# Causal attention with a 64-row tail before two feed-forward layers: the tail rows padded to 128 in the transposes and the product with the values

## The chip, the cores and the metric

The kernel runs on one core of one Trainium2 chip. The metric is the device time of one execution in microseconds (us), the median of three runs. The engines are TensorE (PE, whose weight loads the trace keeps apart as PEld), VectorE (DVE), ScalarE (ACT) and GpSimd (POOL); SyncE (SP) issues the DMAs.

## The reference

Attention over 4 batches, 8 heads, 576 positions and 64 features per head, with a causal mask and a bias from a running sum of `max(s, 0)`; then two feed-forward layers over the 2304 tokens, 512 to 2048 to 512. All of it is in float32.

```python
def _attn_ref(q, k, v, s):
    scale = 1.0 / np.sqrt(D)
    scores = scale * np.matmul(q, k.transpose(0, 1, 3, 2))
    cum = np.cumsum(np.maximum(s, 0.0), axis=-1)
    bias = -(cum[:, :, :, None] - cum[:, :, None, :])
    scores = np.where(causal, -1000000000.0, scores + np.minimum(bias, 0.0))
    scores = scores - np.max(scores, axis=-1, keepdims=True)
    attn = np.exp(scores)
    attn = attn / (np.sum(attn, axis=-1, keepdims=True) + 1e-09)
    return np.matmul(attn, v)
...
    x = attn_out.transpose(0, 2, 1, 3).reshape(B * S, H * D)
    h = x @ w_in                                  # first layer
    x = (h * np.clip(h + 3.0, 0.0, 6.0) / 6.0) @ w_out
    h = x @ w2_in                                 # second layer
    return (h * (1.0 / (1.0 + np.exp(-h)))) @ w2_out
```

## The kernel before

576 positions are four chunks of 128 and a fifth of 64 (`CH`, line 52). Each head is worked in two parts: part A holds the queries 0 to 255 (chunks 0 and 1), part B the queries 256 to 575 (chunks 2, 3 and 4; chunk 4 has 64 rows). So there are 32 heads of part A (`A0_0` to `A3_7`) and 32 of part B (`B0_0` to `B3_7`), taken in the order A0 A1 A2 B0 A3 B1 B2 B3 (line 198), eight heads each. Most arithmetic on float32 is done with a high and a low half (`th`, `tl`; `xh`, `xl`; `gh`, `gl`), each of a format that TensorE multiplies in one pass.

A head of part B goes through these stages. `score` (line 468) multiplies queries with keys into the PSUM tiles `ps0` to `ps3`. `soft` (487) adds the mask `cmask` and finds the row minimum, on DVE, and writes the rows of chunk c to the tile `pb2`, `pb3` or `pb4`. `expo` (500) takes the exponentials on ACT. `norm` (511) divides by the sums: a small sum and a reciprocal on DVE, then one multiplication per chunk on POOL. `trans` (525) transposes the probabilities on TensorE, so that keys come to lie on partitions. It works by groups of key chunks, `[0, 3]`, `[1, 4]` and `[2]` (line 355); one group fills one of two PSUM banks (`pt0`, `pt1`, `pt2`, from the pool `ps_t`). ACT copies the bank to `th`, and `trans_low` (559) subtracts on DVE and leaves `tl`. `v_high` and `v_low` (435, 442) split the values into `vs`, the first on DVE and the second on POOL. `av` (563) multiplies `vs` with `th` and `tl` into the PSUM tile `po`, chunk of keys by chunk of keys; ACT and DVE move the result on.

What has 64 rows on the contracted side of TensorE: the transposes of `pb4`, whose stationary operand is `pb4` itself (five of the twelve transposes of a head; for key chunk 4 it is 64 by 64), and the two products of `av` for key chunk 4. A row of the trace shows this as `64*128` or `64*64` (rows * columns of the stationary operand).

`slot` (688) writes one head's score stage, the transposes and `av` of the head before, and one step of the first feed-forward layer (`first`, `gate_high`, `gate_low`, `second`: the tiles `ph`, `g`, `gh`, `gl`, `acc`) in one piece of code. The order on each engine is not the order of the code: a scheduler in the compiler sets it, and so it can change wherever an instruction changes. After the last head come the rest of the first layer and the whole second layer, in which no head is worked.

Of the kernel before, what the change touches and what calls it, by code (L numbers as in the profile page):

```python
# [22 lines left out]
def f32(ap):  # L23
    return ap.bitcast(F32)
# [3 lines left out]
def kernel(  # L28
# [42 lines left out]
    make_identity(nc, ident)  # L71


    cmask = cpool.tile([P, NFULL * P + P], F32, tag="cmask", name="cmask")
    nc.gpsimd.memset(cmask, 0.0)
    nc.gpsimd.affine_select(
        out=cmask[:, NFULL * P :], in_=cmask[:, NFULL * P :], pattern=[[-1, P]],
        compare_op=ALU.is_ge, fill=-1e9 / SCALE, base=0, channel_multiplier=1,
    )
    half = cpool.tile([P, 1], F32, tag="half", name="half")  # L80
# [207 lines left out]

    c1 = ctx.enter_context(ExitStack())
    apool = c1.enter_context(tc.tile_pool(name="apool", bufs=1))  # L290
    c2 = c1.enter_context(ExitStack())

    def psum(name, bufs):
# [47 lines left out]
    class Head:  # L341
# [3 lines left out]
        def __init__(self, b, part, h, whole, at):  # L345
            self.b, self.part, self.h, self.whole, self.at = b, part, h, whole, at
            self.slot = at % 2
            self.bh = b * H + h
            self.nm = f"{part}{b}_{h}"
            self.chunks = [c for c in range(NCH) if (CH[c][0] < T1) == (part == "A")]  # L350
            self.q0 = CH[self.chunks[0]][0]
            self.nk = CH[self.chunks[-1]][0] + CH[self.chunks[-1]][1]
            self.nq = self.nk - self.q0
            self.nkc = self.chunks[-1] + 1
            self.groups = [[0, 1]] if part == "A" else [[0, 3], [1, 4], [2]]
            self.prob, self.PT, self.pt, self.pS, self.rest = {}, {}, {}, {}, []
            self.pieces = []
            for c in self.chunks:
                w = CH[c][0] + CH[c][1]
                self.pieces += [(c, 0, w, True)] if w <= 512 else [  # L360
                    (c, 0, w // 2, False), (c, w // 2, w, True)]
# [73 lines left out]
        def v_high(self):  # L435
            if self.whole:
                return
            self.vs = apool.tile([P, self.nkc, 2, D], F32R, tag="vs", name=f"vs{self.nm}")
            for cs, n in self.v_parts():
                copy("v", self.vs[:n, cs, 0, :], self.va[:n, cs, :])  # L440

# [11 lines left out]
        def places(self):  # L453
            self.sums = allsums[self.at % 4]
            self.mx = apool.tile([P, NCH + 1], F32, tag="mx", name=f"mx{self.nm}", bufs=4)
            for c in self.chunks:
                r0, n = CH[c]
                w = r0 + n
                name = f"pb{c}{self.nm}"
                if self.at < 14 and self.at % 4 > 1:  # L460
                    tag = (("qs", "kh"), ("vs", "kl"))[self.at % 4 - 2][c]
                    pb = apool.tile([P, w], F32, tag=tag, name=name)
                else:
                    tag = ("pb2", "pb3", "pb2", "pb3", "pb4")[c]
                    pb = apool.tile([P, w], F32, tag=tag, name=name, bufs=2)
                self.prob[c] = pb
# [20 lines left out]
        def soft(self, i):  # L487

            c, a, z, last = self.pieces[i]
            r0, n = CH[c]  # L490
            m0 = NFULL * P - r0
            pb = self.prob[c]
            nc.vector.tensor_tensor_reduce(
                out=pb[:n, a:z], in0=self.pS.pop(i)[:n, :], in1=cmask[:n, m0 + a : m0 + z],
                scale=-SCALE,
                scalar=BIG if a == 0 else self.mx[:n, i - 1 : i],
                op0=ALU.add, op1=ALU.min, accum_out=self.mx[:n, i : i + 1],
            )

        def expo(self, i):  # L500
            c, a, z, last = self.pieces[i]
            if not last:
                return
            n = CH[c][1]
            pb = self.prob[c]
            nc.scalar.activation(
                pb[:n, :], pb[:n, :], AF.Exp, bias=self.mx[:n, i : i + 1], scale=-1.0,
                accum_out=self.sums[:n, c : c + 1],
            )

        def norm(self):
            sm = self.sums[:, self.chunks[0] : self.nkc]
            nc.vector.tensor_scalar(out=sm, in0=sm, scalar1=1e-9, scalar2=None, op0=ALU.add)
            nc.vector.reciprocal(sm, sm)
            if self.whole:
                return
            for c in self.chunks:
                n = CH[c][1]
                pb = self.prob[c]
                nc.gpsimd.tensor_scalar(  # L520
                    out=pb[:n, :], in0=pb[:n, :], scalar1=self.sums[:n, c : c + 1], scalar2=1.0,
                    op0=ALU.mult, op1=ALU.mult,
                )

        def trans(self, gi):

            pt = bank("t", [P, 512], f"pt{gi}{self.nm}")
            off, evac = 0, []
            for kc in self.groups[gi]:
                k0, kn = CH[kc]  # L530
                start = off
                for c in self.chunks:
                    n = CH[c][1]
                    if c >= kc:
                        nc.tensor.transpose(  # L535
                            pt[:kn, off : off + n], self.prob[c][:n, k0 : k0 + kn],
                            ident[:n, :n],
                        )
                        off += n
                self.PT[kc] = (kn, start, off)  # L540
                if evac and evac[-1][0] == kn:
                    evac[-1] = (kn, evac[-1][1], off)
                else:
                    evac.append((kn, start, off))
            dt = F32 if self.whole else F32R
            tag = ("th", "tl")[self.whole and self.slot]
            hi = apool.tile([P, off], dt, tag=f"{tag}{gi}", name=f"th{gi}{self.nm}")
            self.pt[gi] = []
            if not self.whole:
                lo = apool.tile([P, off], dt, tag=f"tl{gi}", name=f"tl{gi}{self.nm}")  # L550
            for kn, a, z in evac:
                copy("a", hi[:kn, a:z], pt[:kn, a:z])
                if not self.whole:
                    self.pt[gi].append((lo[:kn, a:z], pt[:kn, a:z], hi[:kn, a:z]))
            for kc in self.groups[gi]:
                kn, a, z = self.PT[kc]
                self.PT[kc] = (hi[:kn, a:z],) if self.whole else (hi[:kn, a:z], lo[:kn, a:z])

        def trans_low(self, gi):
            for lo, pt, hi in self.pt.pop(gi):  # L560
# [2 lines left out]
        def av(self):  # L563
            b, h, nm, nq = self.b, self.h, self.nm, self.nq
            p = h // 2
            if self.whole:
                self.av_whole()
                return
            if h % 2 == 0:
                if self.part == "A":  # L570
                    xA[b, p] = apool.tile(
                        [P, T1], F32, tag=f"xA{p}", name=f"xA{b}_{p}", bufs=1
                    )
                else:
                    xB[b, p] = apool.tile(
                        [P, T1], F32, tag=f"xB{p}", name=f"xB{b}_{p}", bufs=2
                    )
                    if b == 0:
                        xZ[p] = apool.tile([P, B * TAIL], F32, tag=f"xZ{p}", name=f"xZ{p}")
            mine, other = (slice(0, D), slice(D, 2 * D))[:: 1 if h % 2 == 0 else -1]  # L580
            if self.part == "A":
                outs = [(xA[b, p], 0, T1)]
            else:
                outs = [(xB[b, p], 0, T1), (xZ[p][:, b * TAIL : (b + 1) * TAIL], T1, nq)]
            po = bank("o", [P, nq], f"po{nm}")
            for kc in range(self.nkc):
                kn = CH[kc][1]
                a = max(CH[kc][0] - self.q0, 0)
                v, o = self.vs[:kn, kc].rearrange("p a d -> p (a d)"), po[:, a:]
                last = len(self.PT[kc]) - 1  # L590
                for i, pT in enumerate(self.PT[kc]):
                    nc.tensor.matmul(  # L592
                        o, v, pT, start=kc == 0 and i == 0, stop=kc == self.nkc - 1 and i == last
                    )
            tmp = apool.tile([P, nq], F32, tag="tl2", name=f"tmp{nm}")
            nc.scalar.copy(tmp[mine, :], po[other, :])
            self.rest = [(x[mine, :], po[mine, a:z], tmp[mine, a:z]) for x, a, z in outs]
# [90 lines left out]
    def slot(cur, p1, p2, nx, loads, mm, tk=(0, 0, 0, 0)):  # L688
# [57 lines left out]
        transposed(2)  # L746
        if mm:
            gate_low(step)
        ticks(tk[3])
        if nx:  # L750
            nx.places()
# [212 lines left out]
```

## Time and profile before

| what | value |
|---|---|
| device time, median of 3 runs | 1087.41 us (1085.73 to 1089.71) |
| the profiled execution's own time | 1087.48 us |
| its span, first to last instruction | 1085.7 us |
| PE busy | 1054.0 us, 97% of the span |
| PEld busy | 943.6 us, 87% |
| DVE, ACT, POOL busy | 599.6, 431.7 and 272.5 us (55%, 40%, 25%) |
| granted TensorE clock, mean | 0.998 of full speed |

The span is what the trace covers; 1.8 us of the execution lie around it. Matmuls are pipelined: one takes some 0.28 us from start to end while the next begins 0.12 us after it, so what one costs in a stream is read from start to start, and a PE that is busy all the time can still be slowed.

### The profile page before, as it was taken

How to read it: one execution, taken by the hardware profiler on the slowest of the kernel's cores; microseconds unless marked ns; L12 is line 12 of the kernel's file. 1: busy time of each engine (PE TensorE's matmuls, PEld its weight loads, DVE VectorE, ACT ScalarE, POOL GpSimd, SP SyncE). 2: the span in 40 equal slices, each digit the busy share in tenths (PEclk: the TensorE clock that was granted, in tenths of full speed). 3: DMA queues.
4: the chain of work that ended last, by engine and by line, in shares of the span. 5: the costliest groups of instructions: out<-in, count | busy, mean ns of one | idle time of the engine just before them, and what ended most of it. 6: DMA issues, size and time to landing. Idle time of an engine off the chain costs nothing.

```text
span 1085.7 us, 18479 instructions
## 1 busy us (share of the span) xinstructions
PE 1054.0 (97%) x6658; PEld 943.6 (87%) x6658; DVE 599.6 (55%) x1549; ACT 431.7 (40%) x965; POOL 272.5 (25%) x436
## 2 busy tenths in 40 slices
PE   4988999999999999999999999999999999999998
PEld 3877899999999988988989999888888888888897
DVE  6799976776777777667754229995311311111111
ACT  5787744454445545445442117763111111111111
POOL 4000133332243344434432013232211211111110
PEclk9999999999999999999999999999999999999999
DMA  4792221222222222211201329620200100010010
GB/s 146 224 335 83 58 69 50 61 60 56 78 57 55 75 61 58 75 50 54 83 13 40 98 72 325 190 75 1 78 1 1 59 1 1 1 39 1 1 39 20
DMA packets 51426, 77.09 MB, mean 71 GB/s; under 512 B 11796, under 2 KB 34312, under 8 KB 51336
## 3 DMA queue, kind: packets, MB, share of 16 engines
q1 hardware_dynamic: 51336, 75.92, 22.6%
q8 instruction: 53, 0.87, 0.3%
q14 instruction: 37, 0.30, 0.1%
HBM read 65.93 MB, written 9.95 MB: 70 GB/s over the span
## 4 chain that ended last, share of the span: by engine, by line
PE 84%; DVE 5%; DMA 5%; POOL 2%; SPq 2%; ACT 1%; issue 1%; DVEq 0%; ACTq 0%; POOLq 0%
PE ph L231 12%; PE ph L233 11%; PE ph L232 11%; PE acc L280 6%; PE acc L281 6%; PE acc L282 6%; PE acc L277 5%; PE acc L276 5%; PE acc L278 5%; PE poB L592 5%; PE pt0B L535 3%; DMA rawo<-in_w1o_dram 2%; PE pt1B L535 1%; DMA rawi<-in_w1i_dram 1%; PE pt2B L535 1%
## 5 line engine op out<-in xcount | busy, mean ns | idle before, releaser
L254 DVE TENSOR_TENSOR gl<-g,gh 128x512 fp32r<-128x512 f32 (+1 forms) x152 | 102.7, 676 | 278.0 <-POOL gh L92 277.9
L92 POOL TENSOR_SCALAR gh<-g 128x512 fp32r<-128x512 f32 x136 | 103.1, 758 | 473.6 <-ACT g L249 303.1
L231 PE MATMUL ph<-xh,wi 128*128 128x256 f32 x576 | 169.1, 294 | 8.1 <-DVE g L245 7.8
L232 PE MATMUL ph<-xl,wi 128*128 128x256 f32 x576 | 165.9, 288 | 0.0
L233 PE MATMUL ph<-xh,wi 128*128 128x256 f32 x576 | 165.7, 288 | 0.0
L276 PE MATMUL acc<-gh,wo 128*128 128x256 f32 x576 | 162.3, 288 | 2.3 <-POOL gh L92 2.2
L277 PE MATMUL acc<-gl,wo 128*128 128x256 f32 x576 | 164.0, 287 | 0.3 <-DVE gl L254 0.2
L278 PE MATMUL acc<-gh,wo 128*128 128x256 f32 x576 | 162.9, 285 | 0.0
L249 ACT ACTIVATE g<-ph 128x512 f32<-128x512 f32 x72 | 42.9, 598 | 284.9 <-PE ph L233 284.8
L231 PEld LDWEIGHTS ph<-xh,wi 128*128 128x128 f32 x576 | 111.2, 193 | 11.6 <-DVE g L245 8.9
L233 PE MATMUL ph<-x2h,wi 128*128 128x512 f32 (+1 forms) x320 | 117.7, 368 | 0.0
L232 PE MATMUL ph<-x2l,wi 128*128 128x512 f32 (+1 forms) x320 | 117.7, 368 | 0.0
L231 PE MATMUL ph<-x2h,wi 128*128 128x512 f32 (+1 forms) x320 | 117.7, 368 | 0.0
L280 PE MATMUL acc<-wo,gh 128*128 128x512 f32 x288 | 112.3, 390 | 0.0
L277 PEld LDWEIGHTS acc<-gl,wo 128*128 128x128 f32 x576 | 109.9, 191 | 2.7 <-DVE gl L254 1.4
L281 PE MATMUL acc<-wo,gh 128*128 128x512 f32 x288 | 112.2, 390 | 0.0
L232 PEld LDWEIGHTS ph<-xl,wi 128*128 128x128 f32 x576 | 111.5, 194 | 0.7
L276 PEld LDWEIGHTS acc<-gh,wo 128*128 128x128 f32 x576 | 108.8, 191 | 3.8 <-POOL gh L92 2.4
L233 PEld LDWEIGHTS ph<-xh,wi 128*128 128x128 f32 x576 | 111.5, 194 | 0.7
L278 PEld LDWEIGHTS acc<-gh,wo 128*128 128x128 f32 x576 | 109.8, 191 | 1.0
L282 PE MATMUL acc<-wo,gl 128*128 128x512 f32 x288 | 101.4, 389 | 0.0
L244 ACT ACTIVATE g<-ph,half 128x512 f32<-128x512 f32 (+1 forms) x80 | 51.3, 642 | 63.2 <-PE ph L233 57.8
(185 smaller groups left out, 2102.6 us busy)
## 6 DMA issues: line engine op xcount, KB each, us to landing
k2B<-in_kT_dram SPq DMA_DIRECT2D x64, 144.0 KB
rawi<-in_w1i_dram SPq DMA_DIRECT2D x16, 512.0 KB
rawo<-in_w1o_dram SPq DMA_DIRECT2D x16, 512.0 KB
rawi<-in_w2i_dram SPq DMA_DIRECT2D x16, 512.0 KB
rawo<-in_w2o_dram SPq DMA_DIRECT2D x16, 512.0 KB
q2B<-in_qT_dram SPq DMA_DIRECT2D x64, 80.0 KB
out_dram<-o SPq DMA_DIRECT2D x18, 256.0 KB
vaB<-in_v_dram SPq DMA_DIRECT2D x32, 128.0 KB
```

Source lines behind the costliest of these rows:

```text
L92: nc.gpsimd.tensor_scalar(out=o, in0=i, scalar1=1.0, scalar2=1.0, op0=ALU.mult, op1=ALU.mult)
L231: nc.tensor.matmul(o, wih[:, cs], xh[c], start=c == 0, stop=False)
L232: nc.tensor.matmul(o, wih[:, cs], xl[c], start=False, stop=False)
L233: nc.tensor.matmul(o, wil[:, cs], xh[c], start=False, stop=c == NDC - 1)
L254: nc.vector.tensor_tensor(out=gl, in0=g, in1=f32(gh), op=ALU.subtract)
L276: nc.tensor.matmul(a, woh[:, cs], gh[:, jj, :], start=b0, stop=False)
L277: nc.tensor.matmul(a, woh[:, cs], gl[:, jj, :], start=False, stop=False)
L278: nc.tensor.matmul(a, wol[:, cs], gh[:, jj, :], start=False, stop=b1)
L280: nc.tensor.matmul(a, gh[:, jj, cs], woh, start=b0, stop=False)
L281: nc.tensor.matmul(a, gh[:, jj, cs], wol, start=False, stop=False)
L282: nc.tensor.matmul(a, gl[:, jj, cs], woh, start=False, stop=b1)
L592: nc.tensor.matmul(o, v, pT, start=kc == 0 and i == 0, stop=kc == self.nkc - 1 and i == last)
```

## The change

The rows 64 to 127 of chunk 4 are filled with zeros once, in two new tiles `last0` and `last1` of 128 by 640 that take the place of `pb4` for heads with an even and an odd number. The transposes of chunk 4 then read all 128 partitions and write 128 columns, of which only 64 are kept: the next transpose of the bank writes over the others. In `vs` the rows 64 to 127 of key chunk 4 are set to zero for each head, by a memset on POOL ahead of `v_high`, and `av` contracts over 128 rows for every key chunk. The groups become `[0, 4]`, `[1]`, `[2]`, `[3]`: four banks are filled instead of three, and one copy and one subtraction cover a whole bank. `cmask` is 512 columns wide instead of 640.

```diff
+    NKP = NCH * P
+    lasts = []
+    for i in range(2):
+        lasts.append(apool.tile([P, NKP], F32, tag=f"last{i}", name=f"last{i}"))
+        nc.gpsimd.memset(lasts[i], 0.0)
...
-            self.groups = [[0, 1]] if part == "A" else [[0, 3], [1, 4], [2]]
+            self.groups = [[0, 1]] if part == "A" else [[0, 4], [1], [2], [3]]
...
+            if self.nkc > NFULL:
+                nc.gpsimd.memset(f32(self.vs[CH[-1][1] :, NFULL]), 0.0)
             for cs, n in self.v_parts():
                 copy("v", self.vs[:n, cs, 0, :], self.va[:n, cs, :])
...
-                if self.at < 14 and self.at % 4 > 1:
+                if n < P:
+                    pb = lasts[self.slot]
+                elif self.at < 14 and self.at % 4 > 1:
...
-            m0 = NFULL * P - r0
+            m0 = -a if z <= r0 else NZ - r0
...
                     if c >= kc:
+
                         nc.tensor.transpose(
-                            pt[:kn, off : off + n], self.prob[c][:n, k0 : k0 + kn],
-                            ident[:n, :n],
+                            pt[:, off : off + P], self.prob[c][:, kc * P : (kc + 1) * P], ident
                         )
                         off += n
...
             hi = apool.tile([P, off], dt, tag=f"{tag}{gi}", name=f"th{gi}{self.nm}")
+            copy("a", hi, pt[:, :off])
...
-            for kn, a, z in evac:
-                copy("a", hi[:kn, a:z], pt[:kn, a:z])
-                if not self.whole:
-                    self.pt[gi].append((lo[:kn, a:z], pt[:kn, a:z], hi[:kn, a:z]))
+                self.pt[gi].append((lo, pt[:, :off], hi))
...
-                kn = CH[kc][1]
                 a = max(CH[kc][0] - self.q0, 0)
-                v, o = self.vs[:kn, kc].rearrange("p a d -> p (a d)"), po[:, a:]
+                v, o = self.vs[:, kc].rearrange("p a d -> p (a d)"), po[:, a:]
...
         transposed(2)
         if mm:
             gate_low(step)
+        transposed(3)
```

How the order on the engines moves is shown at three places of heads of batch 2. First, on TensorE before the change, the end of `av` of head `B2_0` (products with the values, `poB2_0`), the next head's scores `ps2B2_2` and the first transposes of `B2_1`; the last figures are the size of the output.

```order
L592 MATMUL poB2_0_5722<-th0B2_0_5624,vsB2_0_5605 128x192
L592 MATMUL poB2_0_5722<-tl0B2_0_5625,vsB2_0_5605 128x192
L592 MATMUL poB2_0_5722<-th1B2_0_5669,vsB2_0_5605 128x64
L592 MATMUL poB2_0_5722<-tl1B2_0_5670,vsB2_0_5605 128x64
L480 MATMUL ps2B2_2_5763<-kaB2_2_5553,qaB2_2_5552 64x288
...
L535 MATMUL pt0B2_1_5772<-ident_78,pb4B2_1_5551 128x64
L535 MATMUL pt0B2_1_5772<-ident_78,pb3B2_1_5550 128x128
L535 MATMUL pt0B2_1_5772<-ident_78,pb4B2_1_5551 128x64
L535 MATMUL pt1B2_1_5818<-ident_78,pb4B2_1_5551 128x64
L535 MATMUL pt1B2_1_5818<-ident_78,pb4B2_1_5551 64x64
```

On TensorE after the change, the same place: the end of `av` of `B2_0`, the transposes of `B2_1`.

```order
L598 MATMUL poB2_0_5775<-tl3B2_0_5753,vsB2_0_5655 128x192
L598 MATMUL poB2_0_5775<-th0B2_0_5674,vsB2_0_5655 128x64
L598 MATMUL poB2_0_5775<-tl0B2_0_5676,vsB2_0_5655 128x64
L549 MATMUL pt1B2_1_5871<-ident_78,pb2B2_1_5600 128x128
...
L549 MATMUL pt0B2_1_5826<-ident_78,last1_106 128x128 x2
L549 MATMUL pt1B2_1_5871<-ident_78,last1_106 128x128
...
L549 MATMUL pt2B2_1_5896<-ident_78,pb2B2_1_5600 128x128
...
L549 MATMUL pt3B2_1_5905<-ident_78,pb3B2_1_5601 128x128
L549 MATMUL pt3B2_1_5905<-ident_78,last1_106 128x128
```

The products of key chunk 4 come from `th0` and `tl0` now, the transposes of chunk 4 read `last1` with 128 rows, and a fourth bank, `pt3`, is filled after `pt2`. Ahead of the first transposes of `B0_0` and behind the end of the last head the order on TensorE does not move.

Second, on POOL after the change, around the split of the values of `B2_2`:

```order
L533 TENSOR_SCALAR last0_104<-last0_104,sums2_94 64x576
L93 TENSOR_SCALAR gh45_6009<-g45_6008 128x512
L448 MEMSET vsB2_2_5968 64x128
L458 TENSOR_TENSOR vsB2_2_5968<-vaB2_2_5837,vsB2_2_5968 128x4x64
L458 TENSOR_TENSOR vsB2_2_5968<-vaB2_2_5837,vsB2_2_5968 64x64
L93 TENSOR_SCALAR qaB2_4_5915<-q2B2_4_5865 64x320
L533 TENSOR_SCALAR pb2B2_3_5913<-pb2B2_3_5913,sums3_96 128x384
```

The memset stands right ahead of the two subtractions of `v_low`; behind it are `qa` of a later head and the multiplications of `norm`. Before the change the same piece reads:

```order
L520 TENSOR_SCALAR pb4B2_2_5704<-pb4B2_2_5704,sums2_94 64x576
L92 TENSOR_SCALAR gh45_5953<-g45_5952 128x512
L92 TENSOR_SCALAR qaB2_4_5859<-q2B2_4_5812 64x320
L448 TENSOR_TENSOR vsB2_2_5912<-vaB2_2_5784,vsB2_2_5912 128x4x64
L448 TENSOR_TENSOR vsB2_2_5912<-vaB2_2_5784,vsB2_2_5912 64x64
L92 TENSOR_SCALAR gh46_6107<-g46_6106 128x512
```

Here `qa` stood ahead of the split; now it stands behind it.

## Rows read from the trace of the kernel before

**Rows 1.** Page, part 1: busy us (share of the span) xinstructions of each engine

```profile
PE 1054.0 (97%) x6658; PEld 943.6 (87%) x6658; DVE 599.6 (55%) x1549; ACT 431.7 (40%) x965; POOL 272.5 (25%) x436
```

**Rows 2.** Windows: stretch, its us, busy us of each engine, PEclk, DMA share, GB/s

```profile
0.00:135.50 135.50, 110.12 (x657) 99.81 (x658) 116.62 (x365) 98.96 (x243) 19.81 (x63) 0.99 0.53 170
135.50:575.70 440.20, 439.97 (x3266) 404.97 (x3265) 308.83 (x908) 210.37 (x518) 162.81 (x262) 1.00 0.21 61
575.70:1085.70 510.00, 503.95 (x2738) 438.85 (x2738) 174.12 (x277) 122.36 (x206) 89.91 (x111) 1.00 0.16 54
```

**Rows 3.** Timeline of PE, 402 to 418 us: start, us, engine, line, operation, tiles, rows*columns, form

```profile
402.62 0.27 PE L535 MATMUL pt2B<-ident,pb2B 128*128 128x128 f32 x1
402.73 0.27 PE L535 MATMUL pt2B<-ident,pb3B 128*128 128x128 f32 x1
402.94 0.27 PE L535 MATMUL pt2B<-ident,pb4B 64*128 64x64 f32 x1
403.14 0.41 PE L592 MATMUL poB<-tl0B,vsB 128*128 128x320 f32 x1
403.39 0.31 PE L592 MATMUL poB<-th1B,vsB 128*128 128x320 f32 x1
403.53 0.34 PE L480 MATMUL ps0B<-kaB,qaB 68*128 68x384 f32 x1
...
406.81 0.25 PE L592 MATMUL poB<-th0B,vsB 128*128 128x192 f32 x1
406.90 0.27 PE L592 MATMUL poB<-tl0B,vsB 128*128 128x192 f32 x1
407.11 0.29 PE L592 MATMUL poB<-th1B,vsB 64*128 64x64 f32 x1
407.24 0.27 PE L592 MATMUL poB<-tl1B,vsB 64*128 64x64 f32 x1
407.44 0.35 PE L480 MATMUL ps2B<-kaB,qaB 68*64 68x288 f32 x1
...
408.94 0.28 PE L231 MATMUL ph<-xh,wi 128*128 128x256 f32 x1
409.06 0.28 PE L232 MATMUL ph<-xl,wi 128*128 128x256 f32 x1
409.27 0.27 PE L535 MATMUL pt0B<-ident,pb4B 64*128 64x64 f32 x1
409.48 0.33 PE L535 MATMUL pt0B<-ident,pb3B 128*128 128x128 f32 x1
409.74 0.28 PE L535 MATMUL pt0B<-ident,pb4B 64*128 64x64 f32 x1
409.85 0.28 PE L535 MATMUL pt1B<-ident,pb4B 64*128 64x64 f32 x2
410.06 0.39 PE L233 MATMUL ph<-xh,wi 128*128 128x256 f32 x1
410.28 0.28 PE L276 MATMUL acc<-gh,wo 128*128 128x256 f32 x1
...
418.04 0.27 PE L535 MATMUL pt0B<-ident,pb4B 64*128 64x64 f32 x1
```

**Rows 4.** Tile pt0B: count, duration min/median/max in ns, first and last start, form

```profile
L535 PE MATMUL pt0B<-ident,pb4B x64: 271/272/276, 159.8 to 567.1; 64*128 64x64 f32 x64
```

**Rows 5.** Tile poB, the products with tl1B, columns as in Rows 4

```profile
L592 PE MATMUL poB<-tl1B,vsB x64: 272/290/312, 168.2 to 575.7; 128*128 128x320 f32 x32, 64*128 64x64 f32 x32
```

**Rows 6.** Timeline of POOL: the memsets at the start, and one step of norm

```profile
0.73 0.20 POOL masks.py:197 MEMSET ident<- 128x128 f32 x1 [0.29 <-POOLq L945]
0.87 0.64 POOL L75 MEMSET cmask<- 128x640 f32 x1
...
413.94 0.74 POOL L520 TENSOR_SCALAR pb4B<-pb4B,sums 64x576 f32<-64x576 f32 x1
```

**Rows 7.** Timeline of DVE: the subtractions that empty the bank pt1

```profile
411.85 0.61 DVE L561 TENSOR_TENSOR tl1B<-pt1B,th1B 128x320 fp32r<-128x320 f32 x2
```

More of the change, by code (lines that the diff above doesn't have):

```diff
@@ L71 @@
     make_identity(nc, ident)
-    cmask = cpool.tile([P, NFULL * P + P], F32, tag="cmask", name="cmask")
+    NZ = (NFULL - 1) * P
+    cmask = cpool.tile([P, NZ + P], F32, tag="cmask", name="cmask")
     nc.gpsimd.memset(cmask, 0.0)
     nc.gpsimd.affine_select(
-        out=cmask[:, NFULL * P :], in_=cmask[:, NFULL * P :], pattern=[[-1, P]],
+        out=cmask[:, NZ:], in_=cmask[:, NZ:], pattern=[[-1, P]],
         compare_op=ALU.is_ge, fill=-1e9 / SCALE, base=0, channel_multiplier=1,
@@ L490, in soft @@
             r0, n = CH[c]
-            m0 = NFULL * P - r0
+            m0 = -a if z <= r0 else NZ - r0
+            assert m0 + a >= 0 and m0 + z <= NZ + P
             pb = self.prob[c]
@@ L506, in expo @@
             nc.scalar.activation(
-                pb[:n, :], pb[:n, :], AF.Exp, bias=self.mx[:n, i : i + 1], scale=-1.0,
+                pb[:n, : CH[c][0] + n], pb[:n, : CH[c][0] + n], AF.Exp, bias=self.mx[:n, i : i + 1], scale=-1.0,
                 accum_out=self.sums[:n, c : c + 1],
@@ L520, in norm @@
                 nc.gpsimd.tensor_scalar(
-                    out=pb[:n, :], in0=pb[:n, :], scalar1=self.sums[:n, c : c + 1], scalar2=1.0,
+                    out=pb[:n, : CH[c][0] + n], in0=pb[:n, : CH[c][0] + n],
+                    scalar1=self.sums[:n, c : c + 1], scalar2=1.0,
                     op0=ALU.mult, op1=ALU.mult,
@@ L527, in trans @@
             pt = bank("t", [P, 512], f"pt{gi}{self.nm}")
-            off, evac = 0, []
+            off = 0
             for kc in self.groups[gi]:
-                k0, kn = CH[kc]
                 start = off
@@ L535, in trans @@
                         nc.tensor.transpose(
-                            pt[:kn, off : off + n], self.prob[c][:n, k0 : k0 + kn],
-                            ident[:n, :n],
+                            pt[:, off : off + P], self.prob[c][:, kc * P : (kc + 1) * P], ident
                         )
                         off += n
[L540 to L544, printed above, removed]
+                self.PT[kc] = (start, off)
             dt = F32 if self.whole else F32R
@@ L550, in trans @@
                 lo = apool.tile([P, off], dt, tag=f"tl{gi}", name=f"tl{gi}{self.nm}")
-            for kn, a, z in evac:
-                copy("a", hi[:kn, a:z], pt[:kn, a:z])
-                if not self.whole:
-                    self.pt[gi].append((lo[:kn, a:z], pt[:kn, a:z], hi[:kn, a:z]))
+                self.pt[gi].append((lo, pt[:, :off], hi))
             for kc in self.groups[gi]:
-                kn, a, z = self.PT[kc]
-                self.PT[kc] = (hi[:kn, a:z],) if self.whole else (hi[:kn, a:z], lo[:kn, a:z])
+                a, z = self.PT[kc]
+                self.PT[kc] = (hi[:, a:z],) if self.whole else (hi[:, a:z], lo[:, a:z])
         def trans_low(self, gi):
```

## The prediction

> **What bounds the kernel now.** I began with the busy times of the page: TensorE is busy for 97% of the span, the next engine, DVE, for 55% [rows 1]. The second view is the windows, to see whether that holds where the change lies. The heads of part B run from 135.5 us (their first scores) to 575.7 us (their last product, [rows 5]), and in these 440.20 us TensorE is busy for 439.97 at a granted clock of 1.00, while DVE is busy for 308.83 (70%), ACT for 210.37 and POOL for 162.81 [rows 2]. So in this stretch nothing is waited for on TensorE's matmul side: the stretch is as long as its stream of matmuls. What is left to ask is whether the stream itself runs at its pace, and a busy time cannot say that, since matmuls overlap. For this the third view is the timeline of PE, read from start to start.
>
> With 128 rows all along, the starts follow each other at a pace set by the columns: 0.11 us after a transpose of 128 columns (402.62 to 402.73), 0.14 after a product of 320 (403.39 to 403.53), 0.09 after one of 192 (406.81 to 406.90), 0.12 after a feed-forward product of 256 (408.94 to 409.06) [rows 3]. Where a row says `64*128`, the pace breaks: 402.73 to 402.94 is 0.21 instead of 0.11, 402.94 to 403.14 is 0.20, and the first product behind it, with 128 rows again, holds the next up until 403.39, 0.25 instead of 0.14 [rows 3]. It is the same at 407.11 and at 409.27. The extra time stands on both sides of each change between 64 and 128 rows, is nearly constant (0.20 to 0.21 on entry and on exit), and does not depend on whether a 64-row transpose or a 64-row product is at hand. I call a run of neighbouring 64-row matmuls an island.
>
> **What the change takes away.** Every matmul with 64 rows gets 128; the score products had 66, 68 or 128 before and keep them, so no island is left. The price of one island comes from the rows, as the time that passes minus what the same matmuls, padded, would take at the pace above [rows 3].
> - 402.73 to 403.39, around the transpose of `pt2`: 0.66 passes; two transposes and a product of 320 columns take 0.11 + 0.11 + 0.14 = 0.36. Extra 0.30.
> - 406.90 to 407.44, around key chunk 4 of `av`: 0.54 passes. A product of 64 columns and 128 rows is not in this stretch; it costs at least half of 0.06 (64 columns at the pace of 256 in 0.12) and at most the 0.09 of 192 columns. I take 0.06, the middle; the two ends move the sum by 1.9 us either way. So 0.09 + 0.06 + 0.06 = 0.21. Extra 0.33.
> - 409.06 to 410.28, two islands with a 128-row transpose between them: 1.22 passes; padded it is 0.12, five transposes of 0.11 and 0.12, 0.79. Extra 0.43 for two. This holds the growth of the 64 by 64 transpose to 128 by 128.
>
> That is 1.06 us for four islands, 0.265 each. The number of islands: the 64-row transposes of `pt0` are 64 and lie between 159.8 and 567.1 us [rows 4], the last 64-row product starts at 575.7 [rows 5]; counted through the timeline of PE the 224 matmuls with 64 rows form 150 islands, 4.7 for each of 32 heads. 150 x 0.265 = 39.8 us. The same subtraction over all 150, which also takes in the slow matmul behind each exit, gives 42.4 us, and over stretches without an island it leaves under 1% unexplained. With exactly four or five islands a head it would be 34 to 45 us. I take 41.
>
> **What it adds and moves.** Transposes: twelve a head before, twelve after (3 + 1, 3, 3, 2); that they grow is in the sum already. Copies and subtractions: before 512, 320, 64 and 320 columns a head, after 384, 320, 320 and 192; four of each, 1216 columns in all, either way. ACT and DVE gain or lose nothing by which the sum could move.
>
> The memset of `vs` on POOL, 64 by 128: not in the trace; a 128 by 128 memset took 0.20 and one of 640 columns 0.64 [rows 6], so it lies between nothing and 0.20. I take 0.15 a head, 5 us in all, on an engine that is free for 63% of the stretch [rows 2]: hidden. It does add a wait: it stands ahead of `v_low` in POOL's queue and cannot start before the last product of the head before has read `vs`. Behind it are `v_low`, `qa` and the three multiplications of `norm`. `v_low` had to wait for that product before too, by way of `v_high`; so the queue is held where it was held, by 0.15 us more.
>
> The two memsets of `last0` and `last1`: 0.64 each by [rows 6], less 0.13 for a narrower `cmask`: 1.15 us on POOL at the very start, ahead of the small memsets that the first heads' DMAs need. Between 0 (the heads' data come later anyhow) and 1.15; I take 0.5.
>
> A fourth bank: `pt2` needs the bank of `pt0` emptied, `pt3` that of `pt1`. In the order after the change the matmuls between are worth 3.7 to 4.1 us and 4.4 to 4.9 us at the pace above. Before, the later of the two subtractions, `tl1`, was done 2.6 us after the last transposes of both banks started (409.85 to 412.46) [rows 3, 7]. Both fit; nothing is added.
>
> Shorter heads: each of the 32 loses 41 / 32 = 1.3 us of some 11. DVE's share rises to 308.83 / 399 = 77% [rows 2]. New waits must come from chains that have less time now. I allow 1 us.
>
> Sum: 1087.5 (the profiled execution, 0.07 us over the median of the runs) - 41 + 0.5 + 1 = **1048 us**.
>
> **A rule that speaks against it.** The pace says that rows matter: entry and exit cost 0.20 to 0.21 where 0.11 is usual [rows 3]. The Trainium skill, TensorE: Matmul & The Clock Gate, section LDWEIGHTS, says that the time of a weight load goes by its columns and not by its rows. By that alone padding rows would remove nothing. The Trainium skill, TensorEngine Tiling (Array Packing), section Key Properties, says that a change of the tiling mode, which goes with 64 rows, drains TensorE; by that the islands end. The rows side with that second page of the Trainium skill.
>
> **The rivals.**
> 1. *Half the gain is eaten by new waits.* The chain that loses most time runs from the last scores (`ps3`) over DVE, ACT and DVE to POOL's `norm`, whose step for chunk 4 ended at 414.68, 3.36 us before its first transpose at 418.04 [rows 3, 6]. From `ps3` to that transpose the matmuls in the new order are worth 7.6 us at the pace above, where before it was 8.5 and two or three islands, some 9.5. So of 3.4 us about 1.4 are left. If DVE, fuller now, delays the chain by 2 us a head, TensorE waits 0.6 us 32 times: 19 us, 1067 us. For it: DVE at 77% with a queue in strict order. Against it: the order puts the reciprocal right behind the same two subtractions as before.
> 2. *The change does not do what it says.* The gaps are not of the 64 rows but of chunk 4: its operands come late, or its loads are not fetched ahead. Then islands stay, and 32 transposes grow by at most 0.11: 1087.5 + 3 = 1089 to 1091 us. Against it: the products of `av` have the same gap as the transposes, and `pb4` at 418.04 was ready 3.36 us before [rows 3, 6]. The rule on loads above would give this time.
> 3. *Slower: the bank turn.* Four banks a head go through two. If `tl1` came over 4.7 us after its transposes instead of 2.6 [rows 3, 7], `pt3` would wait, and `av` behind it. The change becomes a loss once the wait is over 1.3 us a head, so from 6.0 us on; at 7 us the cost is 2.3 a head, 74 us against 41 gained: 1120 us. The subtraction would have to be 2.7 times as late as it was.
>
> **How the numbers follow.** The forecast has 0.76: a full gain of 36 to 45 us, less 0 to 4 us of starts and waits, so 1042 to 1055 us. Rival 1 has 0.14 (1055 to 1080), rival 2 0.05, rival 3 0.05. To leave out no more than 2 in 10 the range reaches into the first rival: 1042 to 1062 us. A measurement of this kernel can tell about 0.3%, 3.3 us, from no change. Faster by more: 0.76 + 0.14 + 0.01 = 0.91; within: 0.05, nearly all rival 2; slower: 0.04.
>
> **What would show it.** In the trace of the changed kernel no matmul should read `64*`; the transposes of `last0` and `last1` should be followed after 0.11 us; PE should stay busy through a stretch that ends near 535 us instead of 575.7; and from there to the end it should again take 510 us. If rows of PE with a wait for POOL or DVE stand before `pt0B`, it is rival 1; before `pt3B`, rival 3. It would be wrong altogether if starts still lay 0.20 us apart around chunk 4.

## The result and the profile after

The changed kernel takes 1046.54 us (median of four runs, 1046.02 to 1048.05), against 1086.60 us for the kernel before (four runs, 1085.73 to 1089.71). The ratio is 0.963, with a 95% interval from 0.961 to 0.965. The forecast was 1048 us, with a range from 1042 to 1062. The profiled execution took 1046.25 us, 41.2 less than the 1087.48 of the one before.

The first view is the page's part 1 for the changed kernel: busy time, share of the span, instructions.

```profile
span 1044.5 us, 18565 instructions
...
PE 1014.1 (97%) x6658; PEld 935.0 (90%) x6658; DVE 600.5 (57%) x1549; ACT 437.6 (42%) x965; POOL 273.6 (26%) x470
```

PE's share is 97% as it was [rows 1]. The time went, and the share doesn't tell from where. The windows of the changed kernel do, cut at the same first scores (135.50) and where 2738 matmuls are left, as in [rows 2]; the columns are those of [rows 2] too.

```profile
135.50:536.40 400.90, 400.67 (x3265) 397.60 (x3265) 309.66 (x910) 217.32 (x519) 163.50 (x294) 1.00 0.24 67
536.40:1044.50 508.10, 503.54 (x2738) 438.74 (x2736) 173.36 (x274) 121.27 (x204) 88.60 (x111) 1.00 0.16 53
```

The stretch of part B took 440.20 us and takes 400.90 for as many matmuls (3266 and 3265): 39.3 of the 41.2 us were gained here. TensorE is as full in it as before (0.23 us without a matmul in both kernels) and the granted clock is the same 1.00, so the same stream runs faster. The waits of PE from 135 to 545 us are one row, and the kernel before has a wait of the same 0.2 us:

```profile
PE ph L232 <- DVE g L246: 0.2, 1, 0.2
```

The other 1.9 us were gained behind this stretch, where the same 2738 matmuls took 510.0 us and take 508.1. Most of that is one wait of the feed-forward layers for POOL, the only one that the waits of PE list from 530 us on. The first row is the kernel before, the second the changed one:

```profile
PE acc L276 <- POOL gh L92: 2.2, 1, 2.2
PE acc L277 <- POOL gh L93: 0.7, 1, 0.7
```

No head is worked there, and why the wait is shorter was not tried.

Where the speed comes from is seen in PE's timeline, from start to start. The first rows lie around the transpose of chunk 4 into `pt2`, the place of 402.62 in [rows 3]; those behind the gap lie around key chunk 4 of `av`, the place of 406.81.

```profile
407.60 0.28 PE L234 MATMUL ph<-xh,wi 128*128 128x256 f32 x1
407.72 0.27 PE L549 MATMUL pt2B<-ident,pb2B 128*128 128x128 f32 x1
407.83 0.27 PE L549 MATMUL pt2B<-ident,pb3B 128*128 128x128 f32 x1
407.94 0.27 PE L549 MATMUL pt2B<-ident,last 128*128 128x128 f32 x1
407.97 0.39 PE L598 MATMUL poB<-tl0B,vsB 128*128 128x320 f32 x1
408.20 0.31 PE L598 MATMUL poB<-th1B,vsB 128*128 128x320 f32 x1
408.35 0.28 PE L232 MATMUL ph<-xh,wi 128*128 128x256 f32 x1
...
412.52 0.25 PE L598 MATMUL poB<-tl3B,vsB 128*128 128x192 f32 x1
412.61 0.22 PE L598 MATMUL poB<-th0B,vsB 128*128 128x64 f32 x1
412.66 0.28 PE L598 MATMUL poB<-tl0B,vsB 128*128 128x64 f32 x1
412.77 0.33 PE L549 MATMUL pt0B<-ident,pb3B 128*128 128x128 f32 x1
412.94 0.27 PE L549 MATMUL pt1B<-ident,pb2B 128*128 128x128 f32 x1
```

The transpose of `last` starts 0.11 us behind the one before it, where the 64-row one stood 0.21 behind. From it to the second product behind it 0.26 us pass (407.94 to 408.20), a transpose at 0.11 and a product at 0.15; the product's record is shown early, and the sum counts. Before, the two took 0.45 (402.94 to 403.39). In the whole trace no matmul with 64 rows is left.

The `av` rows were not foreseen to the hundredth. The two products of 64 columns take 0.05 and 0.11 us, and the transpose behind them holds the next up for 0.17 instead of 0.11.

### The profile page after: what moved, and what is told of

Its sections match the earlier page's. It is cut to its first block, busy times and chain, and to the rows that moved or that the text cites. A ratio compares the mean times of both kernels' runs of the same rounds, so it can differ in the third digit from the quotient of the medians.

```text
span 1044.5 us, 18565 instructions
## 1 busy us (share of the span) xinstructions
PE 1014.1 (97%) x6658; PEld 935.0 (90%) x6658; DVE 600.5 (57%) x1549; ACT 437.6 (42%) x965; POOL 273.6 (26%) x470
## 4 chain that ended last, share of the span: by engine, by line
PE 88%; DVE 7%; DMA 2%; SPq 1%; ACT 1%; issue 1%; POOL 0%; DVEq 0%; ACTq 0%; POOLq 0%
PE ph L232 12%; PE ph L233 12%; PE ph L234 12%; PE acc L281 6%; PE acc L282 6%; PE acc L283 6%; PE acc L277 6%; PE acc L279 6%; PE acc L278 6%; PE poB L598 4%; PE pt0B L549 1%; PE pt1B L549 1%; PE pt2B L549 1%; DVE magi L153 1%; PE ps1B L492 1%
```

## The experiments

Nine kernels ran. Differences below are taken against the 1046.54 us of the changed kernel; each ratio is against the kernel before, on the same chip.

### One half of the padding undone

The first lets `av` contract over 64 rows again for key chunk 4.

```diff
-                v, o = self.vs[:, kc].rearrange("p a d -> p (a d)"), po[:, a:]
+                kn = CH[kc][1]
+                v, o = self.vs[:kn, kc].rearrange("p a d -> p (a d)"), po[:, a:]
...
-                        o, v, pT, start=kc == 0 and i == 0, stop=kc == self.nkc - 1 and i == last
+                        o, v, pT[:kn, :], start=kc == 0 and i == 0, stop=kc == self.nkc - 1 and i == last
```

> The changed kernel, with key chunk 4 of the product with the values contracted over 64 rows again; the transposes stay padded. The order on TensorE then has 32 islands of 64-row matmuls, one a head. Theory (each change between 64 and 128 rows costs TensorE time): 0.29 to 0.35 us an island, 9 to 11 us, so 1056 to 1058 us, with starts 0.20 us apart before and behind these products. Rival (the gain came from the new groups and the new order): nothing is lost, 1046 to 1048 us.

Measured: 1054.25 us (1053.87 to 1055.38), ratio 0.9705 [0.9688, 0.9721]. It loses 7.7 us, and the time lies under the expected range. Counted in its PE timeline, it has 64 matmuls with 64 rows in 32 islands, so 0.24 us for each. The trace of part B shows a little more: from the first scores to the place where 2736 matmuls are left, TensorE takes 401.1 us in the changed kernel and 409.8 in this one, 8.7 more or 0.27 an island. The place of 412.52 above, in this kernel's PE timeline:

```profile
417.25 0.25 PE L599 MATMUL poB<-tl3B,vsB 128*128 128x192 f32 x1
417.42 0.29 PE L599 MATMUL poB<-th0B,vsB 64*128 64x64 f32 x1
417.56 0.27 PE L599 MATMUL poB<-tl0B,vsB 64*128 64x64 f32 x1
417.76 0.33 PE L549 MATMUL pt0B<-ident,pb3B 128*128 128x128 f32 x1
417.93 0.27 PE L549 MATMUL pt1B<-ident,pb2B 128*128 128x128 f32 x1
```

The same five starts take 0.68 us here and 0.42 in the changed kernel. The entry takes 0.17 instead of 0.09, the pair inside 0.14 instead of 0.05, the exit 0.20 instead of 0.11: 0.26 for this island.

The second leaves `av` padded and transposes chunk 4 from 64 rows into 64 columns.

```diff
-                            pt[:, off : off + P], self.prob[c][:, kc * P : (kc + 1) * P], ident
+                            pt[:, off : off + n], self.prob[c][:n, kc * P : (kc + 1) * P],
+                            ident[:n, :n],
```

> The changed kernel, with the transposes of chunk 4 reading 64 rows and writing 64 columns again; the product with the values stays padded, the groups are the new ones. The order on TensorE has 111 islands. Theory: 0.27 us each, 30 us, so 1074 to 1079 us. Rival (groups and order): 1046 to 1049 us. Together with the run before, the two losses should add up to the whole gain of 40 us within 4 us by the theory.

Measured: 1077.69 us (1076.23 to 1078.41), ratio 0.9917 [0.9902, 0.9932], as expected. It loses 31.2 us, and its 160 transposes of 64 rows stand in 111 islands: 0.28 each. Over the same matmuls of part B it is 430.7 us against 401.1, so 29.6 or 0.27 an island; of the rest of the profiled pair's difference, 1.2 us lie ahead of that stretch and 1.2 behind it. A lone one in its PE timeline:

```profile
408.38 0.27 PE L549 MATMUL pt3B<-ident,pb3B 128*128 128x128 f32 x1
408.59 0.27 PE L549 MATMUL pt3B<-ident,last 64*128 64x64 f32 x1
408.79 0.42 PE L599 MATMUL poB<-tl1B,vsB 128*128 128x320 f32 x1
409.04 0.28 PE L234 MATMUL ph<-xh,wi 128*128 128x256 f32 x1
```

0.21, 0.20, and 0.25 where a product of 320 columns takes 0.15: the pattern of [rows 3], back in a kernel with the new groups and their order. The two halves lose 7.7 + 31.2 = 38.9 us, where the whole change gained 40.1 by the medians. What is left for the grouping and everything else is 1 us, which is less than the 0.3% that can be told. In the traces of part B the halves are 8.7 + 29.6 = 38.3 us of 39.3.

### The groups alone

The kernel before, with the new groups and no padding:

```diff
-            self.groups = [[0, 1]] if part == "A" else [[0, 3], [1, 4], [2]]
+            self.groups = [[0, 1]] if part == "A" else [[0, 4], [1], [2], [3]]
...
         gate_low(step)
+        transposed(3)
         ticks(tk[3])
```

> The kernel before with the new groups of key chunks and the fourth bank, and no padding. The order on TensorE has 156 islands, 5 more than before, and each head has five copies and five subtractions instead of four. Theory: no gain, 1086 to 1090 us. Rival (groups and order make the gain): 1046 to 1065 us.

Measured: 1088.39 us (1087.62 to 1092.01), ratio 1.0023 [1.0013, 1.0033]. Four banks a head and another order on every engine gain nothing; if anything they lose 2 us. By the same count it has 156 islands against 151 in the kernel before (the prediction counted 150), and five more at 0.27 are 1.3 us of that. A bank turn that costs dear (rival 3) would have shown here, if not one that needs the shorter heads of the changed kernel.

### The memset taken away

The changed kernel with one lasting tile for the split values, whose lower rows are set to zero once; some tiles of part A got another buffer so that it finds room.

```diff
+    vkeep = apool.tile([P, NCH, 2, D], F32R, tag="vk", name="vk")
+    nc.gpsimd.memset(f32(vkeep[CH[-1][1] :, NFULL]), 0.0)
...
-            self.vs = apool.tile([P, self.nkc, 2, D], F32R, tag="vs", name=f"vs{self.nm}")
-            if self.nkc > NFULL:
-                nc.gpsimd.memset(f32(self.vs[CH[-1][1] :, NFULL]), 0.0)
+            self.vs = vkeep
...
-                    tag = (("qs", "kh"), ("vs", "kl"))[self.at % 4 - 2][c]
+                    tag = (("qs", "kh"), ("va", "kl"))[self.at % 4 - 2][c]
```

> The changed kernel with one lasting tile for the split values, so that the zeros of its rows 64 to 127 are written once and not for each head; 31 memsets and their wait on GpSimd are gone. Theory (hidden behind TensorE): 1045 to 1048 us, no difference that can be told. Rival (the memset holds GpSimd's queue until the last product of the head before, and TensorE pays for it): up to the 0.26 us of each memset, 8 us, so 1038 to 1043 us.

Measured: 1049.38 us (1048.28 to 1052.24), ratio 0.9662 [0.9647, 0.9678]. Both expectations missed: it is 1.4 us above the range of the theory, and the rival's gain is not there. The first row is the window of part B in this kernel, the second the waits of PE from 130 to 600 us.

```profile
135.50:535.00 399.50, 399.50 (x3246) 396.20 (x3246) 306.87 (x907) 217.54 (x519) 155.21 (x262) 1.00 0.24 67
```

```profile
PE pt0A L549 <- POOL pb1A L533: 1.8, 1, 1.8
```

POOL loses its 32 memsets and 8.3 us of work (294 instructions and 163.50 us in the changed kernel), and TensorE was full with them and is full without them: in part B it does not pay for the memset. What was lost lies ahead of 135.5 us, among heads of part A. By 130 us TensorE had started 623 matmuls, against 620 in the changed kernel; then comes a wait of 1.8 us for POOL that the changed kernel does not have, and by 135.5 us they are 647 against 658. That the new buffers brought the wait is likely but was not tried by itself.

### Dummies: one transpose more, of four shapes

These ask what an island costs by itself, and which property makes it. Each is the changed kernel with one more transpose ahead of each bank of a part B head, 128 in all. It repeats the first transpose of the bank, or a part of it, and is written over at once, so it serves nothing. Of the four lines with a comment each kernel has one, without the comment.

```diff
             off = 0
+            if self.part == "B":
+                k0 = self.groups[gi][0]
+                pb = self.prob[max(k0, self.chunks[0])][:, k0 * P : (k0 + 1) * P]
+                nc.tensor.transpose(pt[:, :P], pb, ident)                            # 128 rows
+                nc.tensor.transpose(pt[:, :64], pb[:64, :], ident[:64, :64])         # or: 64 rows
+                nc.tensor.transpose(pt[:64, :P], pb[:, :64], ident)                  # or: 128 rows, 64 columns
+                nc.tensor.transpose(pt[:, :32], pb[:32, :], ident[:32, :32])         # or: 32 rows
             for kc in self.groups[gi]:
```

> The changed kernel with one more transpose ahead of each bank of a head of part B, of the same chunk that the first transpose reads, written over by it: 128 added transposes of 128 rows and 128 columns that serve nothing. Every theory: 0.11 us each, 14 us, so 1059 to 1062 us. It is the level from which the next three are read.

> The same 128 added transposes, but each reads only the first 64 rows of the same chunk and writes 64 columns; less work, the same place, the same operands and waits. Theory (each change between 64 and 128 rows costs): an island each, 0.66 - 0.25 = 0.41 us by the timeline of before, 52 us, so 1094 to 1101 us. Rival (the gaps of before came from the lateness of chunk 4 or from its place): no more than the 128-row version, 1053 to 1062 us.

> The same 128 added transposes with 128 rows, but only 64 columns of the chunk as the stationary operand. Theory (rows matter, columns of the stationary operand do not; the score products of chunk 4 have 64 columns and show no gap): 0.06 to 0.11 us each, 1054 to 1062 us. Rival (any change of the shape that is loaded stops TensorE): as with 64 rows, 1094 to 1101 us.

> The same 128 added transposes with 32 rows and 32 columns written. Theory (what costs is the change of the row size, not the size): as with 64 rows or a little less, 1090 to 1101 us. Rival (cost goes with the number of rows left out or with the columns written): clearly different from the 64-row version, by over 8 us.

| dummy | time, us (lowest to highest) | ratio to before | added | for each of 128 |
|---|---|---|---|---|
| 128 rows | 1062.01 (1061.21 to 1064.17) | 0.9768 [0.9745, 0.9790] | 15.5 | 0.12 |
| 128 rows, 64 stationary columns | 1061.59 (1061.38 to 1062.62) | 0.9763 [0.9739, 0.9787] | 15.1 | 0.12 |
| 64 rows, 64 columns written | 1092.49 (1091.93 to 1095.41) | 1.0053 [1.0036, 1.0070] | 46.0 | 0.36 |
| 32 rows, 32 columns written | 1087.77 (1087.28 to 1089.02) | 1.0005 [0.9994, 1.0015] | 41.2 | 0.32 |

The dummy with half the rows and half the columns adds three times as much as the full one. Both smaller-row dummies came out a little below their ranges: the 0.41 us expected were read at a place where a product of 320 columns stands behind the exit and holds the next start up by 0.10, while here a transpose stands there and holds it up by 0.06. The three fences are the same place in PE's timeline, with 64 rows, with 64 stationary columns, and with 32 rows; L546 is the dummy.

```profile
413.49 0.28 PE L234 MATMUL ph<-xh,wi 128*128 128x256 f32 x1
413.70 0.27 PE L546 MATMUL pt2B<-ident,pb2B 64*128 64x64 f32 x1
413.90 0.33 PE L553 MATMUL pt2B<-ident,pb2B 128*128 128x128 f32 x1
414.07 0.27 PE L553 MATMUL pt2B<-ident,pb3B 128*128 128x128 f32 x1
414.18 0.27 PE L553 MATMUL pt2B<-ident,last 128*128 128x128 f32 x1
```

```profile
406.86 0.28 PE L234 MATMUL ph<-xh,wi 128*128 128x256 f32 x1
406.98 0.27 PE L546 MATMUL pt2B<-ident,pb2B 128*64 128x128 f32 x1
407.08 0.27 PE L553 MATMUL pt2B<-ident,pb2B 128*128 128x128 f32 x1
407.19 0.27 PE L553 MATMUL pt2B<-ident,pb3B 128*128 128x128 f32 x1
```

```profile
411.08 0.28 PE L234 MATMUL ph<-xh,wi 128*128 128x256 f32 x1
411.29 0.24 PE L546 MATMUL pt2B<-ident,pb2B 32*128 32x32 f32 x1
411.47 0.33 PE L553 MATMUL pt2B<-ident,pb2B 128*128 128x128 f32 x1
411.63 0.27 PE L553 MATMUL pt2B<-ident,pb3B 128*128 128x128 f32 x1
```

With 64 rows the entry takes 0.21, the exit 0.20 and the next start 0.17. Without the dummy the feed-forward product would be followed after 0.12 and the next transpose after 0.11: 0.58 - 0.23 = 0.35 added, the 0.36 of the times. With 64 stationary columns the pace isn't broken at all. With 32 rows it breaks as with 64, and the exit is 0.02 shorter.

The last dummy asks whether the price is one of each matmul or of each change: three of 64 rows side by side.

```diff
+                for j in range(3):
+                    nc.tensor.transpose(pt[:, j * 64 : (j + 1) * 64], pb[:64, :], ident[:64, :64])
```

> As the kernel with one added 64-row transpose ahead of each bank, but with three of them, side by side in the bank: 384 added matmuls, which the order on TensorE gathers into 149 islands. Theory (the price is paid at the change of the row size, and inside an island the pace is 0.11 us): 149 x 0.36 + 235 x 0.11 = 79 us over the changed kernel, 1121 to 1130 us. Rival (each matmul with 64 rows pays by itself): three times the 46 us that one added transpose cost, 138 us, 1180 to 1188 us.

Measured: 1113.67 us (1113.66 to 1115.02), ratio 1.0244 [1.0220, 1.0267]: 67.1 us added. By the matmul it would have been over 130, so the price is one of the change. It is below the range for that too, and the PE timeline says why (x3 are three matmuls in one row):

```profile
416.07 0.40 PE L492 MATMUL ps1B<-kaB,qaB 68*128 68x512 f32 x1
416.30 0.39 PE L495 MATMUL ps1B<-khB,qsB 128*128 128x512 f32 x1
416.62 0.40 PE L547 MATMUL pt2B<-ident,pb2B 64*128 64x64 f32 x3
416.95 0.33 PE L554 MATMUL pt2B<-ident,pb2B 128*128 128x128 f32 x1
417.12 0.27 PE L554 MATMUL pt2B<-ident,pb3B 128*128 128x128 f32 x1
```

Three take 0.33 us to the exit where one takes 0.20, so each further one adds 0.065 on average, not the 0.11 of a 128-row transpose that the expectation took. The 384 form 149 islands in this kernel: 149 x 0.36 + 235 x 0.065 = 69 us, near the 67.1 measured.

## Why the prediction was right

**The bound.** "As long as its stream of matmuls" held. TensorE stayed full and 39.3 of the 41.2 us came out of part B's stretch, which was said to end near 535 and ends at 536.4, where as many matmuls are left as at 575.7 before. Two details differ. The last head ends at 528.1 us (the last row of `poB`), since 68 feed-forward products now stand behind it that stood ahead. And what follows was said to take 510 us again and takes 508.1: this gain was not foreseen, and no island lies there.

**The islands, 41 us.** They brought 39.3 us in the profiled pair. A count of the trace of before gives 151 islands (the prediction has 150), so 0.26 each against 0.265 from four places; the 39.8 us that the prediction worked out from those four was nearer than the 41 it took. The two halves undone give 38.9 us for 143 islands, 0.27 each. That the whole still fell by 41.2 is in part luck: 1.7 us less from the islands and 1.5 allowed for starts and waits but not needed about cancel, and the 1.9 behind part B came on top.

**The other reading of the gaps.** Rival 2, that chunk 4 comes late, is refuted by the dummies: the full dummy and that of 64 rows read the same tile at the same place, and the second costs 0.24 us more. The Trainium skill, TensorE: Matmul & The Clock Gate, section LDWEIGHTS, has the rule that a weight load takes its time by columns and not by rows. The trace agrees for the load itself, as these loads of `pt0B` in the kernel before show (lowest, median and highest in ns):

```profile
L535 PEld LDWEIGHTS pt0B<-ident,pb3B x64: 137/138/144, 153.7 to 566.8; 128*128 128x128 f32 x64
L535 PEld LDWEIGHTS pt0B<-ident,pb4B x64: 134/136/140, 159.8 to 567.1; 64*128 64x128 f32 x64
```

A load of 64 rows takes 136 ns in the median and one of 128 takes 138. So the prediction need not have set that rule against the rows: it can hold and the islands still cost, since their time is lost between matmuls of two row sizes, of which the rule says nothing.

**Which property counts.** The prediction took the Trainium skill's page TensorEngine Tiling (Array Packing), section Key Properties, for it: a change of the tiling mode drains TensorE. The trace fits that for rows (0.21 and 0.20 us, entry and exit), though it shows late starts and not the draining itself. The same page lists 128 by 64 as a mode too, in its section Tiling Modes; a stationary operand of 128 rows and 64 columns broke no pace (1061.59 against 1062.01 us), so a narrow stationary operand did not behave here as a change of mode. Every matmul of 64 rows here also had 64 moving columns, but those alone do not break the pace: the padded `av` products with 128 rows and 64 columns are entered after 0.09 us (412.52 to 412.61), as is usual behind 192 columns. More than 64 moving columns on 64 rows were not tried.

**The 64-column product, mis-sized.** Taken at 0.06 us each, a pair takes 0.16, and the transpose behind it then holds the next start up by 0.06: 0.10 us a head more than thought. On the other side the 0.54 us read from the kernel before stop at the exit and leave out the late start behind it, 0.19 (407.44 to 407.63) where 0.14 is usual behind 288 columns. So the `av` islands are worth 0.33 - 0.10 + 0.05 = 0.28 by that place, and 0.26 or 0.27 in the kernel that has only them, and not 0.33. It is some 2 us in all.

**The memset, mis-sized but hidden.** The tile `vs` has this row, with lowest, median and highest in ns:

```profile
L448 POOL MEMSET vsB<- x32: 199/206/367, 147.6 to 519.1; 64x128 f32 x32
```

The median of 0.206 lies just over the bound of 0.20. It costs TensorE nothing in part B, as the kernel without it shows.

**Starts and waits.** 0.5 us was allowed for the two larger memsets at the start. The wait of the first scores is 12.3 us where it was 12.23, so they cost at most 0.1. 1 us was allowed for new waits; none came in part B, since the 0.2 that stands there stood there before too. ACT's work in part B grew, from 210.37 to 217.32 us, and TensorE did not wait for it.

**Rival 1, the chain through `norm`.** POOL's and PE's timelines have the step for chunk 4 and the first transposes of it here:

```profile
409.89 0.75 POOL L533 TENSOR_SCALAR last<-last,sums 64x576 f32<-64x576 f32 x1
413.05 0.38 PE L549 MATMUL pt0B<-ident,last 128*128 128x128 f32 x2
```

The step ends at 410.64, so 2.4 us are left, where 1.4 was worked out and 3.36 had been; the medians over the heads are 2.5 and 3.1. DVE is busy for 309.66 of 400.90 us, 77%, as forecast. The chain got tighter, as said, and did not get late.

**Rival 3, the bank turn.** No wait stands ahead of `pt2B` or `pt3B`, and the groups alone cost 2 us at most.

## What to carry to other kernels

Where TensorE's stream mixes matmuls of 128 rows with some of 64 or 32, count the changes of row size and not the small matmuls: here each trip to 64 rows and back cost some 0.27 us beyond the padded work, and padding with zeros got it back. Putting the small ones side by side should save changes too, since further ones in an island added only 0.065 us each, but no kernel here was made faster that way. A TensorE that is busy for 97% of the time does not show this; read starts against starts around the odd shape. Zeros that must be written again for each head cost nothing here, on an engine that TensorE did not wait for; no run tried it on a busier one.

## What the runs showed of the hardware that was not expected

- The entry is not a constant 0.20 us, as the prediction read it, but some 0.1 more than the pace behind what stands ahead: 0.17 or 0.21 where 0.09 is usual behind 192 columns (417.25 to 417.42; 406.90 to 407.11 in [rows 3]), 0.21 where 0.12 is behind 256, and 0.32 (416.30 to 416.62) where 0.23 is behind 512 (416.07 to 416.30).
- Inside an island a further 64-row transpose adds only 0.065 us on average, less than a 128-row one (0.11).
- The change back delays the next start but one too, by 0.06 us behind a transpose (0.17 for 0.11) and by 0.10 behind a product of 320 columns (0.25 for 0.15).
- 32 rows cost about what 64 do (0.32 and 0.36 us for an added dummy), while the score products with 68 rows stand in the stream at its usual pace: 403.53 in [rows 3] follows 0.14 us behind a product of 320 columns.
- The start behind the transpose that follows two 64-column products of 128 rows is as late (0.17, 412.77 to 412.94), with no change of rows. Why was not tried.
